# Four small loads behind the last piece of w2, on the sync queue of a one-core decode block

## The chip, the core and the metric

The kernel runs on one core of a Trainium2 chip. Its time is the device time of one execution in microseconds (us); the kernel before takes 134.14 us, the median of three runs (134.13, 134.14 and 134.31). A profile, taken by the hardware profiler on one execution, shows each engine's instructions and each queue's transfers against the span, which begins with the first instruction and ends with the last.

The engines are TensorE (PE, matmuls; PEld is its weight load), VectorE (DVE), ScalarE (ACT), GpSimd (POOL) and SyncE (SP). SP and ACT issue the transfers: each has a queue of its own, q1 for SP and q10 for ACT, and both queues are worked off by the same 16 DMA engines.

## The reference

One token for each of two batch rows goes through a layer norm, and then through an attention block and a dense block whose results are added to the input:

```python
xn = _layernorm(x)                                   # x: (2, 1, 576)
# attention: 32 query heads, 16 key/value heads of 128, the last W = 2048 of 8192 positions
q = (xn @ wq)                                        # wq: (576, 4096)
scores = einsum("bhqd,bhkd->bhqk", q, k) * 128 ** -0.5
o = einsum("bhqk,bhkd->bhqd", softmax(scores), v)
A = o.reshape(2, 1, 4096) @ wo                       # wo: (4096, 576)
# dense block, squared relu
h = relu(xn @ w1 + b1) ** 2                          # w1: (576, 4608)
B = h @ w2 + b2                                      # w2: (4608, 576)
out = x + A + B
```

All tensors are bf16. Two rows of activations meet 53.6 MB of caches and weights, each byte of which is used once.

## The kernel before, in words

**Stages.** The attention is cut into eight units u = 0 to 7 (four groups of four key/value heads, times two batch rows). A unit has one tile of k and one of v, each 128 partitions by 16 KB, 2 MB together over all partitions. `step(u)` (line 387) transposes the k tile on TensorE (lines 97 and 262), copies the result out on ScalarE and VectorE (lines 270 and 272), and forms scores and softmax; the product with v of the unit two steps earlier is woven in. `q_block` (line 226) makes the queries from wq before unit 0's scores; `mlp_h` (line 356) makes the hidden layer from w1 between unit 6 and unit 7. After unit 7 everything is summed in one PSUM tile, out_ps: `out_acc` (line 216) multiplies 32 row blocks of wo (line 446), 18 blocks of the first half of w2 (w2a, line 448) and 18 of the second half (line 451), four matmuls for each block. Line 456 copies out_ps to SBUF, and line 457 stores it to the output.

**The loads.** All big loads are issued by SP, in this order: k_0, wq, k_1, v_0, k_2, v_1, k_3, v_2, k_4, v_3, k_5, v_4, k_6, v_5, w1, k_7, v_6, v_7, wo, w2a, w2b, and then w2c in three pieces of 6, 2 and 1 row blocks (line 441, `W2P`). w2b is the first 9 blocks of the second half of w2 and w2c the last 9. k and v tiles share six buffers (`kvpool`); wq, w1 and wo share one. A load into a buffer in use waits for the work that reads it. ACT issues the load of x at the start (line 125), the small loads of b1 (line 418) and b2 (line 419), and two stores to the output. The first of these (line 455) sends a slice of w2b, waits for w2b alone, and is overwritten by the second (line 457), which waits for the first one's landing and for the copy of line 456.

**The completion semaphores.** The framework gives the loads and stores of SP and ACT eight completion semaphores, 0 to 7, which it hands out in turn along the program as it is scheduled. A transfer that takes a semaphore over waits, on its issuing queue, until the semaphore's former user has landed. Each landing adds 16. For the last transfers the hand-out is:

```
semaphore   7     0    1     2     3       4             5       6       7
transfer    v_7   wo   w2a   w2b   w2c 1   early store   w2c 2   w2c 3   final store
```

Here v_7 is the last of one round and the others follow it; the third piece of w2c takes semaphore 6 after v_6.

**The end of the program.** SP closes the program (line 483): it waits for every semaphore and for the other engines, in five wait instructions of two semaphores each and a drain, in a fixed order, and then the engines meet in a barrier and the semaphores are cleared. The five waits are

```
(3, 2)   (4, 1)   (5, 0)   (6, VectorE)   (7, ScalarE)   drain (GpSimd)
```

Each of them waits for the last value that its semaphores will have.

**The tiles.** Pools lie one behind the other in each partition of SBUF: const first, then kvpool, wbig, w2pool, ktpool, work and keep. A `const.tile` with a name of its own gets bytes of its own, and what is added to const moves all later pools up. The k and v tiles start on multiples of 512 B, wo too, w2a 128 B past a multiple of 256.

Of the kernel before, what the change touches and what calls it, by code (L numbers as in the profile page):

```python
# [9 lines left out]
BF16 = mybir.dt.bfloat16  # L10
# [6 lines left out]
def kernel(  # L17
# [14 lines left out]
    nc = tc.nc  # L32
# [51 lines left out]
    const = ctx.enter_context(tc.tile_pool(name="const", bufs=1))  # L84
# [95 lines left out]
    for t0, half, k0, n, pc in ((0, 0, 0, NK, 0), (0, 1, 0, NK, 1), (1, 0, 1, NK - 1, 1), (1, 1, 0, NK - 1, 0)):  # L180
# [11 lines left out]
                          in_=own[:].unsqueeze(2).to_broadcast([P, NC, WC]))  # L192
# [11 lines left out]
                          in_=ident[0:2 * NG4, 0:2 * NG4].rearrange("p (x g) -> p x g", g=NG4).unsqueeze(3)  # L204
# [53 lines left out]
    def transposes(u, g):  # L258
        k_f = k_tiles[u][:].bitcast(F32)
        kT_ps = psum.tile([P, JG * P], BF16, tag="kT", bufs=3, name=f"kT_ps_{u}_{g}")  # L260
        kT_f = kT_ps[:].bitcast(F32)
        for i in range(JG // 2):
            j = g * JG // 2 + i
            transpose(out=kT_f[:, i * P:(i + 1) * P], in_=k_f[:, j * P:(j + 1) * P], identity=ident_f[:])
        t, o = divmod(g, TG)
        if o == 0:
            kT_tiles[(u, t)] = ktpool.tile([P, TG * JG * P], BF16, tag="kT_sb", name=f"kT_{u}_{t}")
        kT = kT_tiles[(u, t)][:, o * JG * P:(o + 1) * JG * P]
        if g % 2 == 0:
            nc.scalar.copy(out=kT, in_=kT_ps[:])  # L270
        else:
            nc.vector.tensor_copy(out=kT, in_=kT_ps[:])  # L272

    def scores(u, t):
        tq, b = divmod(u, B)
        if t == 0:
            sc_tiles[u] = psum.tile([P, NJJ * 32], F32, tag="sc", bufs=2, name=f"sc_ps_{u}")
            matmul(sc_tiles[u][:], lhsT=far_h[:], rhs=is_h, start=True, stop=False, skip_group_check=True)
        sc_ps = sc_tiles[u]
        kT = kT_tiles.pop((u, t))[:].rearrange("p (j k c) -> p j k c", k=P, c=2)  # L280
        z = QZ * (1 - t)
        for c in range(2):
            for g in range(4):
                matmul(sc_ps[32 * g:32 * (g + 1), :], lhsT=qz[:, tq, b, c, z:z + SR],
                       rhs=kT[:, :, 32 * g:32 * (g + 1), c], start=False, stop=(t == NT - 1 and c == 1),
                       skip_group_check=True, tile_position=(0, 32 * g))

    def softmax(u):
        sc_ps = sc_tiles.pop(u)
        m1 = work.tile([P, 1], F32, tag="m1", name=f"m1_{u}")  # L290
        nc.vector.tensor_reduce(out=m1[:], in_=sc_ps[:], axis=AX.X, op=ALU.max)  # L291
        m2 = work.tile([P, NC], F32, tag="m2", name=f"m2_{u}")
        nc.vector.tensor_scalar(out=m2[:], in0=off[:], scalar1=m1[:, 0:1], scalar2=None, op0=ALU.add)  # L293
        gmax = work.tile([P, NC], F32, tag="gmax", name=f"gmax_{u}")
        nc.gpsimd.partition_all_reduce(gmax[:], m2[:], channels=P, reduce_op=ReduceOp.max)  # L295
        gown = work.tile([P, NC], F32, tag="gown", name=f"gown_{u}")
        bias = work.tile([P, 1], F32, tag="bias", name=f"bias_{u}")
        nc.vector.scalar_tensor_tensor(out=gown[:], in0=gmax[:], scalar=-scale, in1=own[:], op0=ALU.mult,  # L298
                                       op1=ALU.mult, accum_out=bias[:])
        p_sb = work.tile([P, NJJ * 32], BF16, tag="p_sb", bufs=1, name=f"p_{u}")  # L300
        o1 = keep.tile([P, Dh + 1], F32, tag="o1", name=f"o1_{u}")
        nc.scalar.activation(out=p_sb[:], in_=sc_ps[:], func=ACT.Exp, bias=bias[:, 0:1], scale=scale,  # L302
                             accum_out=o1[:, Dh:Dh + 1])
        pT = keep.tile([P, NJJ, SR], BF16, tag="pT", name=f"pT_{u}")
        nc.vector.transpose(out=pT[:].rearrange("p j r -> p (j r)"), in_=p_sb[:])  # L305
        pT_tiles[u] = pT
        o1_tiles[u] = o1
# [6 lines left out]
    def pv(u, part, parts):  # L314
        n = NJJ // parts
        if part == 0:
            o_tiles[u] = psum.tile([P, NS * Dh], F32, tag="o", name=f"o_ps_{u}")
        v = v_tiles[u][:].rearrange("p (t j s d) -> p j t s d", t=NT, s=2, d=Dh)
        for j in range(part * n, (part + 1) * n):
            g = j % 4  # L320
            matmul(o_tiles[u][32 * g:32 * (g + 1), :], lhsT=pT_tiles[u][:, j, :], rhs=v[:, j], start=(j < 4),
                   stop=(j >= NJJ - 4), skip_group_check=True, tile_position=(0, 32 * g))
        if part == parts - 1:
            pT_tiles.pop(u)

    def pv_end(u):
        tq, b = divmod(u, B)
        o_ps = o_tiles.pop(u)
        o1 = o1_tiles.pop(u)
        for k in range(NS):  # L330
            kw = dict(out=o1[:, 0:Dh], in0=o_ps[:, k * Dh:(k + 1) * Dh])
            if k == 0:
                nc.vector.tensor_scalar(scalar1=in_s[:, 0:1], scalar2=None, op0=ALU.mult, **kw)
            else:
                nc.vector.scalar_tensor_tensor(scalar=in_s[:, k:k + 1], in1=o1[:, 0:Dh], op0=ALU.mult, op1=ALU.add,  # L335
                                               **kw)

        def fin():
            op = psum.tile([P, Dh + 1], F32, tag="op", name=f"op_ps_{u}")
            pp = slice(32 * tq, 32 * (tq + 1))  # L340
            matmul(op[pp, :], lhsT=of_h[:], rhs=o1[:], start=True, stop=True, skip_group_check=True,
                   tile_position=(0, 32 * tq))
            linv = work.tile([P, 1], F32, tag="linv", name=f"linv_{u}")
            nc.vector.reciprocal(out=linv[pp, :], in_=op[pp, Dh:Dh + 1])
            om_t = work.tile([P, Dh], F32, tag="om", name=f"om_{u}")
            om = om_t[pp, :].rearrange("p (q r) -> p q r", r=WR)
            nc.vector.scalar_tensor_tensor(out=om, in0=op[pp, 0:Dh].rearrange("p (q r) -> p q r", r=WR),
                                           scalar=linv[pp, 0:1], op0=ALU.mult, op1=ALU.mult,
                                           in1=own_c[pp, :].unsqueeze(2).to_broadcast([32, WC, WR]))
            with nc.allow_low_precision(reason="sums of one term and zeros"):  # L350
                nc.vector.tensor_reduce(out=ws[pp, :, BS * b], in_=om.rearrange("p q r -> p r q"), axis=AX.X,  # L351
                                        op=ALU.add)

        return fin
# [32 lines left out]
    def step(u):  # L387
        fin = None
        w = u - 2
        with_pv = w >= 0  # L390
        for g in range(NG):
            transposes(u, g)
            if with_pv and g == 1:
                pv(w, 0, 2)
            if with_pv and g == 2:
                pv(w, 1, 2)
                fin = pv_end(w)
            if g == TG + 1:
                scores(u, 0)
            if g == TG + 2 and fin:  # L400
                fin()
        scores(u, 1)
        softmax(u)

    def pv_all(u):
        pv(u, 0, 1)
        pv_end(u)()
# [31 lines left out]
    nc.sync.dma_start(out=w2b_sb[:], in_=w2_rows[1, :, 0:R9 * D])  # L439
    for r0, r1 in W2P:  # L440
        nc.sync.dma_start(out=w2c_sb[:, (r0 - R9) * D:(r1 - R9) * D], in_=w2_rows[1, :, r0 * D:r1 * D])
    step(NU - 1)
    pv_all(NU - 2)
    pv_all(NU - 1)
# [43 lines left out]
```

## Time and profile before

| what | value |
|---|---|
| median of three runs | 134.14 us (134.13 to 134.31) |
| profiled execution, span | 132.1 us, 2285 instructions |
| profiled execution, around its span | not in the profile; the median of the runs is 2.0 us above the span |
| moved by the DMA engines | 53.76 MB, mean 407 GB/s over the span |
| busy: TensorE, VectorE, ScalarE, GpSimd | 64%, 48%, 35%, 4% of the span |
| first piece of w2c landed, last matmul begun on it | 127.86 us, 129.0 us |
| final store issued | 129.60 us |

Times in the profile are microseconds from the span's start unless ns is written. The page cuts the span into 40 slices and gives the busy share of each in tenths (9 is 90% or more). The chain is the work that ended last, followed back from the end; its shares are of the span. A line of the wait list names who waited, for whom, the total, how often, and the longest. "SPq" and "ACTq" are the instruction queues of these engines, where transfers are issued and semaphores waited for. L94 is line 94 of the kernel, a helper through which all matmuls go, so tiles tell them apart.

### The profile page before, as it was taken

The page shows a single profiled execution, that of the slowest core. Times are in us where ns is not written, and L with a number is a line of the kernel's source. Part 1 is how long each engine was busy: PE and PEld are TensorE (multiplying, and loading weights), DVE is VectorE, ACT ScalarE, POOL GpSimd, SP SyncE. Part 2 cuts the span into 40 slices and gives each one's busy share as a digit, 9 for nine tenths or more (in the row PEclk, how much of TensorE's full clock was granted, in tenths as well). Part 3 has the DMA queues.
Part 4 walks back from the last instruction along what each step waited for, and adds up shares of the span by engine and source line. Part 5 has one row for each costly group of instructions (what it writes and reads, how often), then busy time and mean ns, then how long its engine had stood idle before and what let it go on. Part 6 is the DMA issues. An engine that isn't in the chain of part 4 may idle for free.

```text
span 132.1 us, 2285 instructions
## 1 busy us (share of the span) xinstructions
PE 84.6 (64%) x949; PEld 52.6 (40%) x949; DVE 63.2 (48%) x176; ACT 46.7 (35%) x67; POOL 4.9 (4%) x15
## 2 busy tenths in 40 slices
PE   0089319599589687697599787104819972739471
PEld 0069202286345353363455443002417640229360
DVE  7764400344557677396547687410075667550000
ACT  5725400339566085283256094200106632000000
POOL 5000000010010100100100100100000001000000
PEclk9999955959999999999779999855695999555955
DMA  4999899999999999999999999999999999899960
GB/s 160 397 437 526 369 388 442 422 432 432 429 432 422 442 417 427 437 432 437 432 427 414 437 488 402 445 424 405 427 427 442 468 435 458 376 408 418 418 255 1
DMA packets 3511, 53.76 MB, mean 407 GB/s; under 512 B 419, under 2 KB 558, under 8 KB 814
## 3 DMA queue, kind: packets, MB, share of 16 engines
q1 hardware_dynamic: 3456, 53.61, 95.2%
q8 instruction: 7, 0.11, 0.3%
q10 hardware_dynamic: 46, 0.02, 0.1%
q14 instruction: 2, 0.02, 0.0%
HBM read 53.62 MB, written 0.00 MB: 406 GB/s over the span
## 4 chain that ended last, share of the span: by engine, by line
DMA 78%; PE 15%; ACT 2%; SPq 1%; DVE 1%; issue 1%; ACTq 0%; DVEq 0%
DMA w<-in_B_w_dram 25%; DMA w2c<-in_B_w_dram 24%; DMA k<-in_A_k_cache_dram 16%; DMA wq<-in_A_wq_dram 13%; PE kT_ps L97 5%; PE h_ps L94 3%; PE q_ps L94 3%; PE sc_ps L94 2%; PE out_ps L94 1%; PE o_ps L94 1%; ACT kT L270 1%; DVE qrow L238 1%; SPq L106 0%; ACT qrow L238 0%; DVE qz L254 0%
## 5 line engine op out<-in xcount | busy, mean ns | idle before, releaser
L97 PE MATMUL kT_ps<-ident_f,k 128*128 128x128 f32 x256 | 41.4, 312 | 5.7 <-DMA k<-in_A_k_cache_dram 3.9
L97 PEld LDWEIGHTS kT_ps<-ident_f,k 128*128 128x128 f32 x256 | 32.9, 161 | 18.8 <-issue 9.9
L270 ACT COPY kT<-kT_ps 128x1024 bf16<-128x1024 bf16 x32 | 31.9, 1012 | 17.8 <-PE kT_ps L97 17.8
L272 DVE COPY kT<-kT_ps 128x1024 bf16<-128x1024 bf16 x32 | 21.8, 682 | 6.4 <-PE kT_ps L97 6.1
L94 PE MATMUL sc_ps<-kT,qz 128*32 128x512 bf16 x128 | 9.9, 388 | 6.7 <-DVE kT L272 4.7
L302 ACT ACTIVATE p<-sc_ps,bias 128x512 bf16<-128x512 f32 x8 | 5.5, 688 | 21.4 <-DVE gown L298 18.2
L94 PE MATMUL o_ps<-v,pT 128*32 128x512 bf16 x128 | 11.2, 429 | 0.0
L94 PEld LDWEIGHTS <-xnT 128*4 128x4 bf16 x108 | 3.5, 121 | 16.8 <-issue 15.2
L94 PE MATMUL h_ps<-w,xnT 128*4 128x288 bf16 x72 | 4.3, 429 | 8.0 <-DMA w<-in_B_w_dram 8.0
L305 DVE STREAM_TRANSPOSE pT<-p 128x512 bf16<-128x512 bf16 x8 | 5.7, 710 | 6.2 <-ACT p L302 6.2
L335 DVE SCALAR_TENSOR_TENSOR o<-o_ps,in_s,o 128x128 f32<-128x128 f32 x24 | 8.3, 345 | 0.4
L291 DVE TENSOR_REDUCE m<-sc_ps 128x1 f32<-128x512 f32 x8 | 5.5, 692 | 4.8 <-PE sc_ps L94 4.8
L375 DVE TENSOR_TENSOR hrow<-t 100x1152 bf16<-100x1152 f32 x2 | 2.6, 1355 | 9.6 <-ACT t L373 9.6
L94 PE MATMUL q_ps<-wq,xnT 128*4 128x512 bf16 x36 | 4.0, 627 | 4.9 <-DMA wq<-in_A_wq_dram 4.9
L295 POOL PARTITION_ALL_REDUCE gmax<-m x8 | 2.9, 367 | 104.9 <-DVE m L293 104.9
L94 PE MATMUL op_ps<-o,of_h 128*32 128x129 f32 x16 | 3.7, 316 | 4.6 <-DVE o L335 4.6
L456 ACT CAST fin_sb<-out_ps 113x144 bf16<-113x144 f32 x1 | 0.3, 280 | 17.9 <-PE out_ps L94 17.9
L94 PEld LDWEIGHTS <-qz 128*32 128x32 bf16 x128 | 2.1, 94 | 10.4 <-DVE kT L272 7.2
L97 PE MATMUL pro_ps<-ident,xn_sb 2*128 2x2 bf16 x5 | 0.9, 182 | 6.8 <-DVE xn_sb L171 6.5
L94 PEld LDWEIGHTS <-hT_sb 128*17 128x17 bf16 x144 | 3.4, 108 | 3.6 <-issue 3.5
L94 PE MATMUL out_ps<-wo,ws 128*17 128x144 bf16 x128 | 4.0, 325 | 1.2 <-DVE ws L351 1.2
L238 DVE CAST qrow<-q_ps 100x512 bf16<-100x512 f32 x1 | 0.7, 692 | 8.2 <-PE q_ps L94 8.2
(71 smaller groups left out, 57.4 us busy)
## 6 DMA issues: line engine op xcount, KB each, us to landing
k<-in_A_k_cache_dram SPq DMA_DIRECT2D x8, 2048.0 KB, 21.0
v<-in_A_v_cache_dram SPq DMA_DIRECT2D x8, 2048.0 KB, 21.5
w<-in_B_w_dram SPq DMA_DIRECT2D x1, 5184.0 KB
wq<-in_A_wq_dram SPq DMA_DIRECT2D x1, 4608.0 KB, 17.8
wo<-in_A_wo_dram SPq DMA_DIRECT2D x1, 4608.0 KB
w2a<-in_B_w_dram SPq DMA_DIRECT2D x1, 2592.0 KB, 26.9
w2b<-in_B_w_dram SPq DMA_DIRECT2D x1, 1296.0 KB
w2c<-in_B_w_dram SPq DMA_DIRECT2D x1, 864.0 KB
```

The lines of the kernel that those rows point to most:

```text
L94: tc.keep_in_program_order(nc.tensor.matmul(*a, **k))
L97: tc.keep_in_program_order(nc.tensor.transpose(*a, **k))
L238: cp(out=qrow[:, k * QW:(k + 1) * QW].rearrange("p (i a d) -> p i a d", a=2, d=Dh), in_=q_ps[0:RB, k * QW // 2:(k + 1) * QW // 2].rearrang ...
L270: nc.scalar.copy(out=kT, in_=kT_ps[:])
L272: nc.vector.tensor_copy(out=kT, in_=kT_ps[:])
L291: nc.vector.tensor_reduce(out=m1[:], in_=sc_ps[:], axis=AX.X, op=ALU.max)
L295: nc.gpsimd.partition_all_reduce(gmax[:], m2[:], channels=P, reduce_op=ReduceOp.max)
L302: nc.scalar.activation(out=p_sb[:], in_=sc_ps[:], func=ACT.Exp, bias=bias[:, 0:1], scale=scale, accum_out=o1[:, Dh:Dh + 1])
L305: nc.vector.transpose(out=pT[:].rearrange("p j r -> p (j r)"), in_=p_sb[:])
L335: nc.vector.scalar_tensor_tensor(scalar=in_s[:, k:k + 1], in1=o1[:, 0:Dh], op0=ALU.mult, op1=ALU.add, **kw)
L375: nc.vector.tensor_tensor(out=h4[:, :, k * HB:(k + 1) * HB], in0=t4, in1=t4, op=ALU.mult)
L456: nc.scalar.copy(out=fin_sb[:], in_=out_ps[:])
```

## The change

Behind the loop that issues the three pieces of w2c, SP issues four more loads, each of 64 B a row, on 3, 6, 9 and 12 partitions. Each goes into a tile of 16 partitions by 32 bf16 of its own in the const pool. Nothing reads the tiles.

```diff
     for r0, r1 in W2P:
         nc.sync.dma_start(out=w2c_sb[:, (r0 - R9) * D:(r1 - R9) * D], in_=w2_rows[1, :, r0 * D:r1 * D])
+    for n in (3, 6, 9, 12):
+        t = const.tile([16, 32], BF16, name=f"side_{n}")
+        nc.sync.dma_start(out=t[0:n, :], in_=B_w2[0:n, 0:32])
     step(NU - 1)
```

The order of the instructions on TensorE, VectorE, ScalarE and GpSimd is as before; SP has four more. The const pool is 4 x 64 B = 256 B longer, and all tiles of the later pools stand 256 B higher. The four loads take four semaphores:

```
semaphore   7        0        1        2         3
transfer    side_3   side_6   side_9   side_12   final store
```

The closing waits of SP keep their order and their pairs.

## The prediction

> **What bounds the kernel now.** I read the page's DMA rows and shares of the chain first, because they say whether work on the engines can matter at all. The DMA row has its 40 slices, digits in tenths; the queue row has packets, MB and share.
>
> ```profile
> span 132.1 us, 2285 instructions
> ...
> DMA  4999899999999999999999999999999999899960
> ...
> q1 hardware_dynamic: 3456, 53.61, 95.2%
> ...
> DMA 78%; PE 15%; ACT 2%; SPq 1%; DVE 1%; issue 1%; ACTq 0%; DVEq 0%
> ```
>
> The sync queue's loads (q1) keep the 16 DMA engines full from the second slice to the 38th, and DMA is 78% of the chain. So the stream of weights and caches sets the time up to its last piece, and what the engines do before that is covered. The change stands behind that piece, so next I read the chain in order of time (start, length, what) where it ends:
>
> ```profile
> 96.74 31.12 DMA w2c<-in_B_w_dram
> 127.86 0.04 issue
> 127.90 1.36 PE out_ps L94 x36
> 129.27 0.02 issue
> 129.29 0.28 ACT fin_sb L456
> ```
>
> The reader is to see the serial tail: first piece of w2c landed at 127.86, 36 matmuls to 129.26, copy to 129.57, then the store. The timeline has the two stores on ACT's queue:
>
> ```profile
> 125.80 0.65 ACTq L455 DMA_DIRECT2D out_dram<-w2b  x1
> ...
> 129.60 0.54 ACTq L457 DMA_DIRECT2D out_dram<-fin_sb  x1
> ```
>
> Then the waits of the sync queue (total, times, longest):
>
> ```profile
> SPq L483 <- DMA w2c<-in_B_w_dram: 27.4, 3, 26.8
> ...
> SPq L441 <- DMA v<-in_A_v_cache_dram: 3.1, 1, 3.1
> SPq L483 <- DMA out_dram<-fin_sb: 2.3, 1, 2.3
> ...
> SPq L483 <- DMA out_dram<-w2b: 0.3, 1, 0.3
> ```
>
> Two things are in it. The third piece of w2c, though nothing overwrites its buffer, stood 3.1 us behind v_6: it takes over v_6's completion semaphore (6). And the end of the program (L483) is SP waiting for every DMA in turn, the final store last: 2.3 us, from the landing of w2c's third piece at 128.92 to 131.23. Last, the instructions of L483 (min/median/max in ns, first and last start):
>
> ```profile
> L483 SPq EVENT_SEMAPHORE  x7: 17/28/28, 127.9 to 132.0; - x7
> L483 POOLq EVENT_SEMAPHORE  x4: 17/17/17, 131.4 to 131.9; - x4
> L483 SPq DRAIN  x3: 7/7/13, 131.3 to 131.6; - x3
> ```
>
> The same view, cut to stretches of a few ns, places them: SP's wait on the final store runs at 131.237, its drain at 131.302, the next drain at 131.366. So SP starts one such instruction every 64 to 65 ns, although they last 7 to 28. GpSimd's pair at 131.399 and 131.476 is 77 apart. From 131.237 to the end of the span, some 0.8 us, nothing runs but this closing.
>
> **The change, part by part.**
>
> *The four issues on SP.* In the order of the built program each load takes the next semaphore and waits for its former user: side_3 for v_7, side_6 for wo, side_9 for w2a, side_12 for w2b. TensorE reads w2a from 122.73, and the early store, which waits for w2b alone, starts at 125.80; so side_12 goes out at about 125.80 and the others before. An issue costs SP between 0.25 us (the smallest of the two-partition b1 loads on ACT) and 0.65 (the early store); I take 0.43, w2c's. SP has nothing to issue after its last w2c piece (100.74 + 0.33) and its first closing wait was passed only at 127.88. side_12 is through by 125.80 + 0.65 = 126.45. Nothing is queued behind but the closing waits. Cost 0, hidden by 1.4 us of SP waiting; with that cover gone it would be 0.43 us.
>
> *The bytes.* 30 rows of 64 B are 1.9 KB against 53.76 MB: at the page's mean of 407 GB/s, 5 ns. They stand on q1 behind all of w2c, which was issued by 101.1, so on each DMA engine they come after the pieces that the chain waits for. How long a tiny load takes is bounded by two rows. The x load on two partitions was issued at 0.73, and SP's k_1, which waits for it, went at 2.19: 1.46 us. The final store, issued at 129.60, is seen by SP at 131.237: 1.64 us. From 125.80 these give 127.3 to 127.4; behind w2c, which is all landed at 128.92, a load that began only then would land at 130.4 to 130.6. Both are before 131.22. And the DMA engines are empty then: the windows (last two columns DMA share and GB/s) read
>
> ```profile
> 128.00:129.00 1.00, 1.00 (x36) 0.89 (x33) 0.00 (x0) 0.00 (x0) 0.00 (x0) 0.50 0.17 59
> 129.00:130.00 1.00, 0.24 (x8) 0.05 (x3) 0.00 (x0) 0.28 (x1) 0.00 (x0) 0.50 0.00 0
> ```
>
> Cost 0; the cover is the final store's own landing, with 0.6 to 2.3 us to spare. The early store, issued in the same instant as side_12, has room too: it landed at 128.26 (the 0.3 us wait) and is wanted at 129.60.
>
> One rule speaks against this step. The Trainium skill, "DMA: Bandwidth & Descriptors", section "Measured", calls transfers under 64 KB descriptor-dominated, and its section "Rules for kernel authors" wants them merged. If four such loads each paid that page's roughly 2 us one after another on the path (an estimate from its fixed cost, fitted there for another issuing engine), the kernel would end near 142 us; they are on no path here, so I give it nothing.
>
> *The closing waits.* The semaphores go round in eights, so four more loads move the final store from semaphore 7 to 3. SP's closing list keeps its order and its five double waits: (3, 2), (4, 1), (5, 0), (6, VectorE), (7, ScalarE), then the drain. Before, the first four passed at 127.88, 128.26, 128.56 and 128.92, under the tail, and only the fifth waited for the final store. Now the first one waits for it, and the other four, each satisfied, come after it on the path. No row shows two satisfied waits on SP one behind the other, so I bound the price: from below their own length, 4 x 28 = 0.11 us, if they run back to back; from above GpSimd's spacing, 4 x 77 = 0.31. Nothing lets it be a gain, as four instructions are added to a serial end. I take SP's own spacing from wait to drain, the nearest row: 4 x 65 = 0.26 us.
>
> The Trainium skill, "Perfetto Trace Analysis", section "Sequencer-only Instruction (DRAIN, etc)", says that the profiler shows only the execution of such an instruction, not fetch, decode or the push of its update. By the durations alone the sum would be 0.11; with that rule the spacing is what counts, which is what the rows at 131.237, 131.302 and 131.366 show.
>
> *The tiles.* The four tiles take 256 B of each partition, and every tile after the const pool (k and v, weights, work tiles) stands 256 B higher. Do positions matter? w2a starts 128 B past a multiple of 256 and wo on a multiple of 512, and the stream ran at 429 GB/s in the stretch 116 to 122, where w2a comes in, against 423 at 95 to 100 with k and v tiles on multiples of 512. Matmuls on w2c start their rows at many offsets and lie within 278 to 328 ns. Taken as 0; the ends are 1.4% of the stream either way, from the gap of 429 to 423: about 1.8 us.
>
> **Sum.** 132.1 (the span) + 0.26 = 132.4 us for the profiled execution. The span lies 2.0 us under the median of the runs, 134.14 (134.13 to 134.31), for what lies around the span, which the change leaves alone. So 134.14 + 0.26 = 134.40 us, +0.19%. The 0.2% bound, about what a measurement of this kernel can tell from no change, is 134.41: the forecast falls almost on it.
>
> **The rivals.**
> - *Nothing is paid.* If SP had the four waits ready and ran them in the shadow of the first, the time stays 134.14 to 134.2. For it: each lasts 28 ns at most. Against: SP's drains were ready as well and still came 64 ns apart. 5 in 100.
> - *The side loads hold up w2c.* Place: the rings of q1 between 122.7 and 128.9. The third piece landed at 128.92 and the last four of the 36 matmuls need it at about 129.1, so a delay of its landing costs us for us from 0.2 us on; the first piece has no slack at all. Price: one issue time per load on the stream, 0.43 us for side_12 alone, 134.14 + 0.26 + 0.43 = 134.8, or 1.2 us for the three late ones, 135.6. For it: three issues fall into the last 11 us of the stream. Against: they stand behind w2c. 18 in 100, with a side load that lands after the final store counted here.
> - *The shift pays.* With all tiles 256 B higher the stream runs up to 1.4% faster, which decides from 0.26 us of gain on, 0.2% of the stream: 134.40 - 1.8 = 132.6 at the far end, 134.14 at the near one. For it: 99% of the span hangs on DMA writes into shifted tiles. Against: the rates above. 7 in 100. This is the case that is not slower.
>
> **How the numbers follow.** The forecast (134.25 to 134.45 by its bounds) has 70 in 100. It straddles 134.41, so with the scatter of the runs (0.18 us) I give 34 of these to slower and 36 to within 0.2%. Slower: 34 + 18 = 52. Same: 36 + 5 = 41. Faster: 7. The range takes in the forecast with its bounds, the unpaid case below and the lower end of the second rival above, with the runs' scatter: 134.05 to 134.80.
>
> **What would show it.** Right: SP's first closing wait ends with the final store and four more follow 65 ns apart ahead of the drain, so that the time from the store's issue to the span's end grows from 2.5 us (129.60 to 132.1) to about 2.75; all before 129.60 stands. The wait list then puts one long wait on the final store or on side_12. Wrong: a later start of the w2c matmuls than 127.90 (second rival), an earlier one by over 0.26 us (third), closing waits under 30 ns apart (first), or the first closing wait ended by side_12's landing later than the store's.

## The result and the profile after

The kernel with the four loads takes 134.31 us, the median of eleven runs (134.12 to 134.51); the kernel before, run beside it, takes 134.0 us (eleven runs, 133.89 to 134.31). The ratio of the runs is 1.0018, with a 95% interval of 1.0011 to 1.0026, that is 0.15 to 0.35 us slower; the medians alone lie 0.31 us (0.23%) apart. The interval does not hold 1, so the loss is there, but it reaches to both sides of the 0.2% bound.

The page after the change shows the same picture of the stream:

```profile
span 132.6 us, 2289 instructions
...
DMA  4999899999999999999999999989999999999950
...
q1 hardware_dynamic: 3516, 53.61, 94.9%
```

Sixty packets more on q1 are the 30 rows of the four loads and their 30 semaphore writes. The span is 0.5 us longer than the one before. This execution took 134.46 us, one of the slower of the eleven, whose spans go from 132.2 to 132.6. The chain's end and ACT's two stores show where its half microsecond lies:

```profile
96.34 31.80 DMA w2c<-in_B_w_dram
128.14 0.04 issue
128.18 1.36 PE out_ps L94 x36
129.54 0.02 issue
129.56 0.28 ACT fin_sb L459
```

```profile
126.08 0.64 ACTq L458 DMA_DIRECT2D out_dram<-w2b  x1
129.56 0.28 ACT L459 CAST fin_sb<-out_ps 113x144 bf16<-113x144 f32 x1 [17.21 <-PE out_ps L94]
129.87 0.54 ACTq L460 DMA_DIRECT2D out_dram<-fin_sb  x1
```

Here the first piece of w2c landed at 128.14, 0.28 us later than in the profile before, and everything to the final store's issue (129.87 for 129.60) moved along. w2b, which lies ahead of w2c, was already as much later (the early store, 126.08 for 125.80), before any row of the new loads had moved. In the profiles of the experiments below whose tiles stand on the same places, the matmuls on w2c start between 127.88 and 128.14, with and without loads in the tail, against 127.90 before and 128.18 here, so I take this part for scatter of the stream. The runs agree: the median of the spans is 132.4 for the change and 132.1 to 132.2 for the kernel before in the runs beside the experiments, 0.2 to 0.3 us in all. The other part lies behind the final store. SP's instructions of the closing line:

```profile
L486 SPq EVENT_SEMAPHORE  x7: 17/27/28, 131.5 to 132.5; - x7
...
L486 SPq DRAIN  x3: 7/7/13, 131.8 to 132.1; - x3
```

Before, the first of the seven started at 127.9 and the first drain at 131.3. Now all seven start at 131.5 or later, and the first drain comes at 131.8. Their start times, to the ns, from the trace's instruction records:

```
                 wait 1    wait 2    wait 3    wait 4    wait 5    drain
before          127.879   128.264   128.561   128.922   131.237   131.302
after           131.504   131.574   131.641   131.705   131.767   131.832
```

From the wait that ends with the final store to the drain it is 0.065 us before and 0.328 after: 0.263 us more. The wait list of SP after the change:

```profile
SPq L444 <- DMA wo<-in_A_wo_dram: 10.8, 1, 10.8
...
SPq L444 <- DMA w2a<-in_B_w_dram: 5.9, 1, 5.9
SPq L486 <- DMA out_dram<-fin_sb: 5.1, 1, 5.1
SPq L444 <- DMA v<-in_A_v_cache_dram: 4.5, 1, 4.5
...
SPq L444 <- DMA w2b<-in_B_w_dram: 2.8, 1, 2.8
```

The four issues (L444) waited for v_7, wo, w2a and w2b, whose semaphores they took over, and then SP stood 5.1 us on the final store, where it used to pass four waits meanwhile.

### The profile page after: what moved, and what is told of

It is laid out like the page before. It is cut to its first block, busy times and chain, and to the rows that moved or that the text cites. A ratio compares the mean times of both kernels' runs of the same rounds, so it can differ in the third digit from the quotient of the medians.

```text
span 132.6 us, 2289 instructions
## 1 busy us (share of the span) xinstructions
PE 82.4 (62%) x949; PEld 50.3 (38%) x949; DVE 63.3 (48%) x176; ACT 46.9 (35%) x67; POOL 4.9 (4%) x15
## 4 chain that ended last, share of the span: by engine, by line
DMA 78%; PE 15%; SPq 1%; DVE 1%; ACT 1%; issue 1%; ACTq 0%; DVEq 0%
DMA w<-in_B_w_dram 25%; DMA w2c<-in_B_w_dram 24%; DMA k<-in_A_k_cache_dram 16%; DMA wq<-in_A_wq_dram 13%; PE kT_ps L97 6%; PE h_ps L94 3%; PE q_ps L94 3%; PE sc_ps L94 2%; PE out_ps L94 1%; PE o_ps L94 1%; DVE qrow L238 1%; SPq L106 0%; ACT qrow L238 0%; DVE qz L254 0%; SPq L438 0%
## 5 line engine op out<-in xcount | busy, mean ns | idle before, releaser
L97 PE MATMUL kT_ps<-ident_f,k 128*128 128x128 f32 x256 | 40.7, 307 | 7.5 <-DMA k<-in_A_k_cache_dram 6.3
L97 PEld LDWEIGHTS kT_ps<-ident_f,k 128*128 128x128 f32 x256 | 31.7, 157 | 21.8 <-issue 14.0
L94 PE MATMUL sc_ps<-kT,qz 128*32 128x512 bf16 x128 | 10.4, 410 | 6.7 <-DVE kT L272 4.7
L94 PE MATMUL h_ps<-w,xnT 128*4 128x288 bf16 x72 | 3.8, 391 | 7.3 <-DMA w<-in_B_w_dram 7.3
L333 DVE TENSOR_SCALAR o<-o_ps,in_s 128x128 f32<-128x128 f32 x8 | 2.8, 346 | 4.6 <-PE o_ps L94 4.6
L94 PEld LDWEIGHTS <-hT_sb 128*17 128x17 bf16 x144 | 2.8, 98 | 4.8 <-issue 4.6
```

The lines of the kernel that those rows point to most:

```text
L94: tc.keep_in_program_order(nc.tensor.matmul(*a, **k))
L97: tc.keep_in_program_order(nc.tensor.transpose(*a, **k))
```

## The experiments

Three theories are to be told apart. *Closing order*: the new loads cost nothing where they stand; they shift the final store from semaphore 7 to 3, and the satisfied waits that now follow it cost 65 ns each. *Loads in the tail*: the loads cost by being there, by their issue, their rows or their landing. *Shift of the tiles*: the cost comes from every later tile standing 256 B higher.

All comparisons are against the kernel before, run beside the others. "Place" is the closing wait, of five, that holds the final store.

| run | small loads mid / tail | later tiles moved by | place | us | against before, 95% interval |
|---|---|---|---|---|---|
| before | 0 / 0 | 0 | 5 | 134.05 | |
| the change | 0 / 4 | 256 B | 1 | 134.31 | 1.0018 (1.0011 to 1.0026) |
| mid_only | 4 / 0 | 256 B | 1 | 134.34 | 1.0017 (1.0007 to 1.0027) |
| mid_and_tail | 4 / 4 | 256 B | 5 | 134.05 | 1.0006 (0.9996 to 1.0016) |
| tiles_only | 0 / 0 | 256 B | 5 | 134.08 | 1.0001 (0.9988 to 1.0014) |
| twelve_tail | 0 / 12 | 256 B | 2 | 135.58 | 1.0114 (1.0098 to 1.0130) |
| sixteen_parts | 0 / 4 | 256 B | 1 | 134.41 | 1.0031 (1.0018 to 1.0044) |
| one_tail | 0 / 1 | 64 B | 3 | 134.87 | 1.0058 (1.0042 to 1.0075) |
| one_tail_256 | 0 / 1 | 256 B | 3 | 134.18 | 1.0010 (1.0001 to 1.0019) |
| seven_mid | 7 / 0 | 256 B | 4 | 138.32 | 1.0306 (1.0289 to 1.0323) |
| three_mid_four_tail | 3 / 4 | 256 B | 4 | 134.11 | 1.0007 (0.9997 to 1.0017) |
| tile_64 | 0 / 0 | 64 B | 5 | 134.69 | 1.0046 (1.0034 to 1.0059) |
| tile_128 | 0 / 0 | 128 B | 5 | 134.55 | 1.0036 (1.0023 to 1.0049) |

The time of before is that of the runs beside the first four experiments; beside the others it was 134.0 to 134.05.

**mid_only.** The loads leave the tail, and the final store keeps semaphore 3.

```diff
+    side = const.tile([P, 128], BF16, name="side")
...
             w1_sb = issue_flat(B_w1, "w1")
+            for i, n in enumerate((3, 6, 9, 12)):
+                p, c = 32 * (0 + i // 4), 32 * (i % 4)
+                nc.sync.dma_start(out=side[p:p + n, c:c + 32], in_=B_w2[0:n, 0:32])
```

> The four small loads stand in the middle of the program, behind the load of w1, and none stands behind w2c; a tile of 256 B in const holds them, so the later tiles stand 256 B higher as in the change. The final store gets completion semaphore 3 as in the change. Closing order: the first closing wait on SP ends with the final store's landing and four satisfied ones follow, 62 to 70 ns apart, so the wait on the final store to the first drain takes 0.33 us (before: 0.065), and the kernel is 0.26 us slower than before, 134.26 against 134.0. Loads in the tail: with nothing behind w2c the cost is gone, 134.0 us. Shift of the tiles: the cost stays at 0.24 to 0.3 us, but ahead of 129.6 us, with one wait after the final store as before.

The cost stayed, with no load behind w2c. SP's closing instructions and its long wait:

```profile
L487 SPq EVENT_SEMAPHORE  x7: 17/28/28, 131.4 to 132.4; - x7
L487 SPq DRAIN  x3: 7/7/13, 131.7 to 132.0; - x3
```

```profile
SPq L487 <- DMA out_dram<-fin_sb: 30.2, 1, 30.2
```

All seven start at 131.4 or later, as in the change: the wait that the final store ends starts at 131.408 and the drain at 131.736, 0.328 us. SP stood 30.2 us on the one wait with nothing else to do. The cost needs no loads in the tail.

**mid_and_tail.** The change's tail is put back beside the four loads in the middle; eight loads bring the final store round to semaphore 7.

```diff
             w1_sb = issue_flat(B_w1, "w1")
+            for i, n in enumerate((3, 6, 9, 12)):
...
         nc.sync.dma_start(out=w2c_sb[:, (r0 - R9) * D:(r1 - R9) * D], in_=w2_rows[1, :, r0 * D:r1 * D])
+    for i, n in enumerate((3, 6, 9, 12)):
+        p, c = 32 * (1 + i // 4), 32 * (i % 4)
+        nc.sync.dma_start(out=side[p:p + n, c:c + 32], in_=B_w2[0:n, 0:32])
```

> The four small loads stand behind w2c as in the change, and four more in the middle of the program, behind w1. With eight loads the final store gets semaphore 7 again, as before the change. The tiles stand 256 B higher. Closing order: four closing waits pass before the final store lands, the fifth ends with it, the drain follows 65 ns later, and the time is that of before within the noise, 134.0 us, although all that the change put into the tail is there. Loads in the tail: slower by 0.24 us as in the change. Shift of the tiles: slower by 0.24 us too.

134.05 us, as before. The same view, cut first to 127 to 130.9 us and then to 131 to 133, shows the closing waits split again:

```profile
L490 SPq EVENT_SEMAPHORE  x4: 28/28/961, 128.2 to 129.3; - x4
```

```profile
L490 SPq EVENT_SEMAPHORE  x3: 17/17/28, 131.5 to 132.2; - x3
L490 SPq DRAIN  x3: 7/7/7, 131.6 to 131.9; - x3
```

Four waits have started by 129.341, under the matmuls, one ends with the store at 131.485, and the drain follows at 131.550. The four loads of the change are all there, and so is the tiles' shift. The interval still admits 0.16%, but the step from the store's wait to the drain is that of before, 65 ns. The four loads in the middle, which mid_only has too, cost nothing here either.

**tiles_only.** The four tiles are allocated, and nothing is loaded.

```diff
+    for i, n in enumerate((3, 6, 9, 12)):
+        t = const.tile([16, 32], BF16, name=f"side_{i}")
```

> The four tiles of the change are allocated and no load is issued: all later tiles stand 256 B higher, the semaphores are those of before. Closing order and loads in the tail: 134.0 us, no difference from before that the interval can tell from zero. Shift of the tiles: slower by 0.24 us, with the landing of w2c some 0.2 to 0.3 us later than 127.9.

134.08 us, ratio 1.0001: moving the tiles by 256 B costs nothing that these runs can tell (up to 0.14% is not excluded).

**twelve_tail.** Where does the cover of the loads end? Twelve loads, each waiting for a semaphore of something that must have landed, push the last ones past the store.

```diff
+    for i, n in enumerate((3, 6, 9, 12, 3, 6, 9, 12, 3, 6, 9, 12)):
+        p, c = 32 * (0 + i // 4), 32 * (i % 4)
+        nc.sync.dma_start(out=side[p:p + n, c:c + 32], in_=B_w2[0:n, 0:32])
```

> Twelve small loads behind w2c in place of four, in one tile of 256 B. Each takes over a semaphore of a transfer that must have landed, so from the fifth on they wait for w2c's pieces and for the first of their own kind: the fifth goes out at 127.9 to 128.1, the seventh at 128.9 to 129.2, and the last five 0.3 us apart, the twelfth at 130.4 to 130.7. With 1.46 us from issue to landing (the x load) it lands at 131.9 to 132.2, after the final store (131.2 to 131.5). The final store has semaphore 4, the twelfth load 3. Closing order, with landing as its limit: the first closing wait ends with the twelfth load, four satisfied ones follow, and the kernel is 0.7 to 1.1 us slower than before. If small loads were hidden however many they are: 0.2 us, the three waits behind semaphore 4.

The direction was right and the size too small: 1.53 us for 0.7 to 1.1. (The landing times expected, 131.9 to 132.2, with four waits of 65 ns behind them make 0.9 to 1.2.) SP's wait list from 125 us on:

```profile
SPq L445 <- DMA w2b<-in_B_w_dram: 2.8, 1, 2.8
SPq L445 <- DMA w2c<-in_B_w_dram: 2.2, 2, 1.8
SPq L487 <- DMA side<-in_B_w_dram: 1.2, 1, 1.2
```

The first closing wait now ends with a small load, not with the store. The twelfth load went out at 130.856 and the wait ended at 132.365: 1.51 us, where the x load had given 1.46. That is 1.13 us after the 131.237 of before; with four satisfied waits of 65 ns it makes 1.39, which is what the span of this profile grew by; the four runs scatter from 135.29 to 135.86. The load went out 0.2 to 0.5 us later than expected, 0.3 us of it because the eleventh took 0.61 us to issue and the others 0.24 to 0.31. Why that one was long I did not find out.

**sixteen_parts.** The same four loads on 16 partitions each.

```diff
+    for i, n in enumerate((16, 16, 16, 16)):
+        t = const.tile([16, 32], BF16, name=f"side_{i}")
+        nc.sync.dma_start(out=t[0:n, :], in_=B_w2[0:n, 0:32])
```

> The four loads of the change on 16 partitions each in place of 3, 6, 9 and 12; the final store has semaphore 3. Closing order: as in the change, 0.26 us slower than before, with four satisfied waits behind the final store. If the odd numbers of partitions mattered (an issue that takes longer, unevenly filled DMA engines): less, 134.05 to 134.2.

Slower by 0.31% (0.18 to 0.44), no less than the change; its closing runs from 131.437 to the drain at 131.764, 0.327 us. The numbers of partitions don't matter for the closing. The median is 0.1 us above the change's; the two intervals overlap.

**one_tail.** One of the four loads alone, to see the price of two waits.

```diff
+    for i, n in enumerate((3,)):
+        t = const.tile([16, 32], BF16, name=f"side_{i}")
+        nc.sync.dma_start(out=t[0:n, :], in_=B_w2[0:n, 0:32])
```

> One of the four loads, the one on 3 partitions, stands behind w2c. The final store gets semaphore 0, which is in the third closing wait. Closing order: two waits pass before the final store lands, the third ends with it, two satisfied ones follow: from the third's start to the drain 3 x 65 = 0.195 us, that is 0.13 us more than before, 134.18 against 134.05. If each load in the tail cost the same, a quarter of the change's 0.24 us: 0.06 us, and one wait after the store.

A miss: 0.86 us slower, about three times the whole change. Two waits do follow the store, as expected (132.046 and 132.108, the drain at 132.173), but the chain shows that the time was lost long before:

```profile
97.11 31.54 DMA w2c<-in_B_w_dram
128.65 0.04 issue
128.69 1.34 PE out_ps L94 x36
```

w2c landed at 128.65. One tile of 64 B moves all later tiles by 64 B, not 256, and the trace's packet records have most packets of 16 KB at 613 ns and more, where before has 611. This had not been varied by the change, and it called for the next three runs.

**tile_64 and tile_128.** No load, semaphores as before; a tile of 64 B, or of 128 B, moves the later tiles.

```diff
+    const.tile([P, 32], BF16, name="side")     # tile_128: [P, 64]
```

> No load is added and the semaphores are those of before; one tile of 64 B in const moves every later tile up by 64 B, as the run with one load did (there the tiles that loads write start 64 B past a multiple of 256, w2a 192). If that position is what made the run with one load 0.86 us slower and not 0.13: 134.5 to 134.7, with the start of the w2c matmuls 0.4 to 0.7 us later than 127.90 and one wait after the final store as before. The trace of the run with one load has 613 ns for a packet of 16 KB where before has 611; 192 such big packets on each DMA engine times 2 ns is 0.4 us. If instead the one load itself did it: 134.0.

> As the run before this, with a tile of 128 B: the tiles that loads write start 128 B past a multiple of 256, except w2a, which comes to stand on one. w2a stood 128 B past a multiple before the change and its packets took 771 ns for 20736 B, as much above bytes over rate as those of wo on a multiple. So if that holds for all: 134.0 and packets of 16 KB at 611 ns. If any offset from 256 costs: 134.5 to 134.7.

Both are slower, by 0.46% and 0.36%, with the store in the last closing wait as before. The windows 20 to 60 and 60 to 100 us (last two columns DMA share and GB/s) of the run with 64 B:

```profile
20.00:60.00 40.00, 32.25 (x291) 18.23 (x280) 22.67 (x58) 19.86 (x29) 1.46 (x4) 0.92 1.01 428
60.00:100.00 40.00, 24.81 (x245) 14.53 (x243) 19.44 (x45) 12.06 (x18) 1.10 (x3) 0.80 1.00 427
```

and of the run whose tiles moved by 256 B:

```profile
20.00:60.00 40.00, 33.61 (x285) 19.06 (x281) 21.95 (x57) 19.57 (x29) 1.47 (x4) 0.85 1.01 429
60.00:100.00 40.00, 23.09 (x250) 13.14 (x243) 19.80 (x46) 12.13 (x18) 1.10 (x3) 0.79 1.01 432
```

With the DMA engines just as busy, 427 to 428 GB/s stand against 429 to 432. Added up from the packet records after the first 10 us, a packet of 16 KB takes 612.3 ns on the mean before, in the change and, within 0.1 ns, in seven runs moved by 256 B, and 615.0 ns at 64 and at 128 B. (seven_mid, further down, was moved by 256 B too and has 614.5, but 612.6 ahead of the gap in its stream.) All packets of q1 of 512 B and more together take 117.5 us of each DMA engine in the former and 117.9 in the latter. That is 0.4 of the 0.5 to 0.64 us. For 128 B I had expected nothing, from w2a, and that was wrong.

The Trainium skill, "DMA: Bandwidth & Descriptors", section "How a descriptor splits into AXI transactions", says that a descriptor is cut into pieces of 256 B, each of which must start on a multiple of 256, so that one which starts elsewhere costs beats for nothing. The runs agree with its direction: 256 B is free, and 64 and 128 B are not. It gives the rule for what is read, and here only the place written moved; and the packets of w2a took 771 ns both at 128 B past a multiple (before) and on one (tile_128), which the rule doesn't explain.

**one_tail_256.** The single load again, with its tile taking 256 B.

```diff
+    side = const.tile([P, 128], BF16, name="side")
...
+    nc.sync.dma_start(out=side[0:3, 0:32], in_=B_w2[0:3, 0:32])
```

> One load on 3 partitions behind w2c as in the run with one load, but its tile takes 256 B of const, so the later tiles keep their place relative to 256 B. Closing order with the position set right: the final store is in the third wait, two satisfied waits follow, 0.13 us slower than before, 134.1 to 134.2. If the one load in the tail costs by itself: 0.8 us, as with the tile of 64 B.

134.18 us, 0.10% slower (0.01 to 0.19), 0.13 us. SP's closing from 131 us on:

```profile
L485 SPq EVENT_SEMAPHORE  x5: 17/28/2626, 128.7 to 132.2; - x5
L485 SPq DRAIN  x3: 7/7/7, 131.5 to 131.8; - x3
```

The third wait, for the pair (5, 0), had semaphore 5 at 128.743 and the store's, 0, at 131.369, and is shown as running 2626 ns between them; waits at 131.406 and 131.467 and the drain at 131.532 follow.

**seven_mid.** Seven loads in the middle, so that one wait follows the store.

```diff
             w1_sb = issue_flat(B_w1, "w1")
+            for i, n in enumerate((3, 6, 9, 12, 3, 6, 9)):
+                p, c = 32 * (0 + i // 4), 32 * (i % 4)
+                nc.sync.dma_start(out=side[p:p + n, c:c + 32], in_=B_w2[0:n, 0:32])
```

> Seven small loads (3, 6, 9, 12, 3, 6 and 9 partitions) stand in the middle of the program behind w1, none behind w2c; one tile of 256 B holds them. The final store gets semaphore 6, in the fourth closing wait. Closing order: one satisfied wait follows it, 0.13 us from the fourth wait's start to the drain, 0.065 us more than before: 134.1 to 134.15, within the noise, although more loads are added than in the change. If the number of small loads set the cost, 7/4 of the change's: 0.4 us, 134.45.

Neither: 4.3 us slower. With seven loads behind w1, k_7 takes over the semaphore of w1 itself and stands behind it:

```profile
SPq L106 <- DMA w<-in_B_w_dram: 12.1, 1, 12.1
```

```profile
88.00:90.00 2.00, 0.00 (x0) 0.00 (x0) 0.00 (x0) 0.00 (x0) 0.00 (x0) 0.50 0.31 126
90.00:92.00 2.00, 0.79 (x16) 0.49 (x19) 0.00 (x0) 0.00 (x0) 0.00 (x0) 0.50 0.01 0
92.00:94.00 2.00, 2.00 (x40) 1.13 (x36) 0.00 (x0) 0.00 (x0) 0.00 (x0) 0.50 0.66 262
```

The stream ran low from 88 us on and dry from 90 to 92, for k_7 was issued only at 91.23, when w1 had landed. The closing, at least, is as expected: the wait on the store at 135.573, one more at 135.634, the drain at 135.699.

**three_mid_four_tail.** Seven loads without that: three in the middle, the change's four in the tail.

```diff
             w1_sb = issue_flat(B_w1, "w1")
+            for i, n in enumerate((3, 6, 9)):
...
+    for i, n in enumerate((3, 6, 9, 12)):     # behind w2c, as in mid_and_tail
```

> Seven small loads again, three in the middle of the program behind w1 and the change's four behind w2c, one tile of 256 B. k_7 now takes over the semaphore of k_5 and not that of w1, so that the stream doesn't run dry as it did with seven in the middle. The final store is in the fourth closing wait. Closing order: one satisfied wait after it, 0.065 us slower than before, 134.05 to 134.15. If the number of loads cost: over 0.24 us.

134.11 us, 0.07% slower with an interval that holds zero. The wait on the store starts at 131.288, one satisfied wait at 131.349, the drain at 131.414. So the series by place, from the store's wait to the drain: 0.065 us at place 5, 0.126 at 4, 0.328 at 1, and at place 3 0.163 from the wait's end (0.191 with the 28 ns that the others' waits last). Place 2 was not seen on its own, as twelve_tail's first wait ends later than its store's. The satisfied waits step by 61 to 70 ns, whatever number of loads stands in the tail. No version ran faster than the kernel before, whose final store stands in the last closing wait already.

## Why the prediction was right, and where its working was not

- *The closing waits* carry the result. Four satisfied waits at SP's own spacing were to cost 0.26 us; measured 0.263 in the profile, and 0.15 to 0.35 in the time. From the store's issue to the end of the span it went from 2.46 to 2.72 us, where about 2.75 was forecast. mid_only has the cost without the loads in the tail, and mid_and_tail the loads without the cost. The spacing, and not the 28 ns that each instruction lasts (0.11 us), was the right row. The forecast of 134.40 stood on a base of 134.14; on the 134.0 of the eleven runs it makes 134.26, against 134.31.
- *The issues on SP*: hidden, as said. They lasted 0.27 to 0.32 us each, where I took 0.43, and the last went out at 126.08, together with the early store.
- *The bytes*: hidden. side_12 landed at 129.35 by the trace's semaphore records, 2.1 us ahead of the store's 131.49. twelve_tail shows the bound from the other side: once a load is issued at 130.86, it ends the kernel.
- *The tiles*: the value taken, 0, was right for 256 B (tiles_only, 134.08 against 134.05). The argument under it was not, so that the term came out right by luck. I read from w2a's rate that 128 B past a multiple of 256 is free, and so that position doesn't matter; tile_128 costs 0.5 us. As far as the runs show, the shift was harmless because 256 B keeps every tile's place relative to 256, and a change with one or two such tiles would have been mispredicted by half a microsecond or more.
- *Nothing is paid* fell: the satisfied waits took 62 to 70 ns each. *The shift pays* fell with tiles_only. *The side loads hold up w2c* fell with mid_and_tail, although the sign that I had named for it, matmuls on w2c later than 127.90, did appear in the profile of the change (128.18): mid_only, with nothing behind w2c, has 128.09 and tiles_only, with no load at all, 128.03, so the start moves by 0.2 us without them too, and the sign was a poor one. Its working also had a slack of 0.2 us for the third piece of w2c that isn't there: by the trace before, that piece landed at 128.905 and the last four matmuls began at 128.947, 0.25 us behind the four ahead of them, where the earlier groups of four follow within 0.13. And three issues of 0.43 us make 1.3, not 1.2.
- *The chances*: the change is 0.18% slower by the ratio of the runs, just under the 0.2% bound (the medians, at 0.23%, lie just over it), as the straddling forecast of +0.19% allowed; the larger chance, 52, had gone to over 0.2%. The interval leaves both open. The 18 points for held-up loads were too many for a case that the order of the queue spoke against.

## What to carry to other kernels

A load that nothing reads still takes its turn in the hand-out of completion semaphores: look at which transfer now waits for whose semaphore, and in which of the closing waits the last store ends up, for each satisfied wait behind it is paid in full (65 ns here). The same hand-out can cost far more in the middle of a stream, where a load may inherit the semaphore of a large one that is still under way (4.3 us in seven_mid). And before an experiment adds a tile, pad it so that the tiles behind keep their place relative to 256 B, or the shift is measured along with it (0.64 us for 64 B).

## What the runs showed of the hardware

- Satisfied semaphore waits on SP start 61 to 70 ns apart, though they are shown as lasting 27 or 28 ns.
- A closing wait for two semaphores is shown from the arrival of the one named first. Where the other comes later, the wait for it is shown as length: 2626 ns in one_tail_256 (pair (5, 0), the store on 0), 961 in mid_and_tail. Where the one named first comes last, it is not: in the change side_12 (2) landed at 129.35 and the store (3) at 131.49, and the wait for (3, 2) is shown from 131.504 with 27 ns.
- The packets of loads take 0.3 to 0.4% longer when their destination tiles start 64 or 128 B past a multiple of 256: 615.0 ns against 612.3 for 16 KB, 117.9 us against 117.5 for all. Why w2a alone, 128 B past, shows none of it is open.
- A load of 64 B a row on 12 partitions took 1.51 us from its issue to the wait that it ended, on nearly idle DMA engines (a share of 0.02 from 130.8 to 132.4 us in twelve_tail).
